# First loads, first weights, last stores: the two ends of a fused cross-covariance attention and MLP kernel rearranged

## The chip, the cores and the metric

The kernel runs on one core of a Trainium2 chip. A core has five engines that run their own instruction streams side by side and wait for each other through semaphores: TensorE (PE, matrix products), VectorE (DVE), ScalarE (ACT, pointwise functions), GpSimd (POOL) and SyncE (SP). Transfers are issued by SP, ACT or POOL and done by 16 DMA engines. The metric is the device time of a run in microseconds, and the number given is the median of the runs.

## The reference

Four batches of q, k and v, each 6080 tokens by 256 features, go through an attention over features, and its output through an MLP with 2048 hidden features:

```python
qn = q / (norm(q, axis=1) + 1e-6)          # over the 6080 tokens
kn = k / (norm(k, axis=1) + 1e-6)
s = kn.transpose(0, 2, 1) @ qn / tau       # 256 x 256 per batch
a = softmax(s, axis=-1)
x = (v @ a).reshape(24320, 256)
out = gelu_tanh(x @ w_in) @ w_out          # 256 -> 2048 -> 256
```

All inputs and the output are float32; `tau` is 1.

## The kernel before

**The algebra.** The norms are taken out of the product: G = q^T k is accumulated over the tokens ("gram"), the sums of squares of q's and k's columns are kept beside it, and the scores are G times a factor per row (from q) and per column (from k). Then v @ a @ w_in is computed as v @ (a @ w_in): A W_in is a 256 x 2048 matrix per batch (`AW`), so that the hidden layer is one product of v^T with it. v^T comes by DMA transposes of a bf16 copy of v (`cast_v`, L133, then `load_vt`, L143), apart from the first two blocks, whose v is turned on TensorE (`pe_vt`, L302).

**Blocks.** Each batch is cut into 12 blocks of 512 tokens (the last has 448), 48 in all (n = 0 to 47). A block computes eight pairs of hidden features: `g0` to `g7` are its products (`mm1`, L486), `G0` and so on their Gelu (`gelu`, L504); some pairs go through a scheme with fewer products (`small`, L544). The second product with w_out is also done with fewer products, on sums of w_out (`prep_wout`, `product`). The order of all this is written out by hand: `ORDER` holds lists of steps, one picked for each block by `WINDOW`, and each engine executes its own instructions in that order. A suffix such as `-1` or `+2` names another block than the current one.

**The start.** Only batch 0's attention can't hide behind other work. Its q and k are read in chunks of token rows: token row r of partition p is token p*47 + r, and a chunk of n rows has n x 128 tokens. Chunk 0 is loaded as float32 by SP and ACT and cast; the later ones are cast to bf16 by POOL's DMAs, one for q and one for k, each 512 KB of bf16 for 8 rows. The sizes are `[8, 7, 8, 8, 8, 6, 2]`, and the second chunk takes the 64 tokens that are left over. For each chunk ScalarE squares q, VectorE squares k, VectorE adds the halves of an 8-row chunk (`fold_rows`, L186), and TensorE sums the squares (`ss_rows`, L234): for q one narrow product per 128 columns and row, for k one 256-column product per row. Then come two 256-column gram products per row (`gram_row`, L219). Between these, `warm` (L341) issues products whose result nobody reads. `WARM` gives their number per chunk.

After the last chunk, `q_factor` (L269) has made q's factor, exp(-0.5 ln(sum of squares)), on ScalarE as soon as q's sums were there; `scores` (L278) makes k's factor in the same way (`lnk`, `rk`), multiplies G by it on VectorE (`S`), and takes the exponential on ScalarE with q's factor as scale (`eT`). `first_aw` (L315) makes the softmax sums and the first 512 features of `AW`; the remaining ones are `aw2` to `aw7`, with copies `ac2` to `ac7`, as steps of block 0. There `aw3` and `aw2` make features 512 to 1023, and need the second quarter of w_in. A load of ScalarE's table for Gelu (L856) follows `first_aw`.

**POOL's queue.** In order: the chunks of q and k, the first v, w_in in four loads of 512 features, the second v, both halves of w_out, then `vb2`, the bf16 copy of block 2's v. POOL's DMAs use eight completion semaphores in turn, so that each waits until the one eight before it has landed; each also waits for its buffer. q and k tiles have five buffers, the tiles of squares, which w_out's halves use too, have two.

**The end.** A block's output tile is stored by four DMAs of 32 partitions each, issued by SP (`store`, L784). The last block is stored in two halves (`store_half`, L773), each by two DMAs of SP and two of ACT. SP's and ACT's DMAs share eight completion semaphores in the same manner; the assignment is made when the program is built. SP's first DMA of block 46 waits for VectorE, its fourth for the semaphore that ACT's first DMA of block 47 uses.

## Time and profile before

| | |
|---|---|
| median of 3 runs | 701.26 us (700.62 to 702.35) |
| the profiled execution | 697.46 us, its span 695.7 us |
| TensorE's granted clock | 0.997 of full speed |
| batch 0's last q and k land | 32.8 and 33.4 us |
| first product of block 0 | 38.59 us |
| last product of block 47 | 688.8 us |
| HBM traffic over the span | 166 GB/s; the DMA engines are full until about 45 us |

Times in the profile are microseconds from the start of the span unless marked ns. In a row of a timeline stand the start, the duration, the engine, the line of the program, the operation, its output and inputs, how many instructions the row holds, and in brackets how long the engine sat idle before it and what released it. A merged row of several instructions overlaps the next where they are pipelined. `PEld` is TensorE's weight load, `SPq` and `ACTq` are DMAs issued by these engines, with the time of the issue only. A row of waits names who waited for whom, the time in all, how often and the longest. The first table of the page gives each engine's busy time; the chain of work that ended last follows the end of the program back from each step to what released it.

### The profile page before, as it was taken

How to read it: one execution, taken by the hardware profiler on the slowest of the kernel's cores; microseconds unless marked ns; L12 is line 12 of the kernel's file. 1: busy time of each engine (PE TensorE's matmuls, PEld its weight loads, DVE VectorE, ACT ScalarE, POOL GpSimd, SP SyncE). 2: the span in 40 equal slices, each digit the busy share in tenths (PEclk: the TensorE clock that was granted, in tenths of full speed). 3: DMA queues.
4: the chain of work that ended last, by engine and by line, in shares of the span. 5: the costliest groups of instructions: out<-in, count | busy, mean ns of one | idle time of the engine just before them, and what ended most of it. 6: DMA issues, size and time to landing. Idle time of an engine off the chain costs nothing.

```text
span 695.7 us, 14290 instructions
## 1 busy us (share of the span) xinstructions
PE 672.1 (97%) x5403; PEld 530.4 (76%) x5479; DVE 631.0 (91%) x1243; ACT 617.0 (89%) x894; POOL 70.2 (10%) x131
## 2 busy tenths in 40 slices
PE   3999999999999999999999999999999999999996
PEld 2756777777777777777777777777777888888885
DVE  4588899999998889999999889999999999999996
ACT  5379999998889999998888999999888999999993
POOL 4321100111001001101010010010000000000000
PEclk9999999999999999999999999999999999999998
DMA  9999996987777976657578787783553464453315
GB/s 243 208 260 130 149 153 120 122 113 95 119 132 120 122 129 113 111 81 128 87 135 121 120 133 119 95 135 58 77 107 62 77 103 73 76 96 59 60 32 88
DMA packets 162277, 79.32 MB, mean 114 GB/s; under 512 B 150464, under 2 KB 153280, under 8 KB 161216
## 3 DMA queue, kind: packets, MB, share of 16 engines
q0 software_dynamic: 13440, 39.46, 34.9%
q1 hardware_dynamic: 147664, 37.67, 33.9%
q10 hardware_dynamic: 1104, 1.28, 0.6%
q8 instruction: 43, 0.70, 0.4%
q14 instruction: 26, 0.21, 0.1%
HBM read 78.91 MB, written 36.83 MB: 166 GB/s over the span
## 4 chain that ended last, share of the span: by engine, by line
PE 89%; DMA 7%; DVE 1%; issue 1%; ACT 1%; POOL 0%; DVEq 0%; POOLq 0%; ACTq 0%
PE r L702 23%; PE h L496 19%; PE p L702 17%; PE rb L572 13%; PE qp L572 10%; PE G L227 5%; DMA t<-in_k_dram 2%; DMA vb<-in_v_dram 2%; DMA t<-in_q_dram 1%; PE awp L436 1%; DMA vT<-vb 1%; PE ss L259 0%; DVE qp L593 0%; PE rk L381 0%; DVE a L191 0%
## 5 line engine op out<-in xcount | busy, mean ns | idle before, releaser
L702 PEld LDWEIGHTS <-wcomb 128*128 128x128 bf16 x2688 | 262.4, 98 | 42.6 <-issue 0.2
L506 ACT ACTIVATE g<-h 128x1024 bf16<-128x1024 f32 (+1 forms) x178 | 179.5, 1013 | 16.1 <-PE h L496 14.2
L702 PE MATMUL r<-t,wcomb 128*128 128x256 bf16 (+1 forms) x1152 | 164.7, 271 | 0.1
L496 PE MATMUL h<-vT,aw 128*128 128x512 bf16 (+1 forms) x582 | 159.5, 376 | 3.5
L598 ACT ACTIVATE g<-qp 128x1024 bf16<-128x1024 f32 (+1 forms) x103 | 104.6, 1016 | 6.1 <-PE qp L572 3.7
L702 PE MATMUL p<-g,wcomb 128*128 128x256 bf16 (+1 forms) x760 | 106.7, 271 | 0.0
L496 PEld LDWEIGHTS <-aw 128*128 128x128 bf16 x712 | 69.4, 98 | 48.8 <-issue 0.7
L572 PEld LDWEIGHTS <-sw 128*128 128x128 bf16 x824 | 80.2, 98 | 27.5 <-issue 0.9
L178 ACT ACTIVATE sq<-t 128x1536 bf16<-128x1536 bf16 (+4 forms) x60 | 80.8, 1361 | 9.5 <-DMA t<-in_q_dram 9.5
L593 DVE TENSOR_TENSOR qp<-rb,yw 128x512 f32<-128x512 f32 (+1 forms) x103 | 71.0, 689 | 12.6 <-PE rb L572 8.6
L572 PE MATMUL rb<-tv,sw 128*128 128x256 bf16 (+1 forms) x412 | 78.0, 271 | 0.4 <-DVE qp L593 0.2
L596 DVE TENSOR_TENSOR xw<-rb,yw 128x512 f32<-128x512 f32 (+1 forms) x103 | 69.6, 676 | 4.6 <-PE rb L572 3.7
L572 PEld LDWEIGHTS <-aw 128*128 128x128 bf16 x618 | 60.4, 98 | 12.7 <-issue 1.2
L588 ACT ACTIVATE qp<-rb 128x512 f32<-128x512 f32 (+1 forms) x103 | 59.8, 580 | 10.4 <-PE rb L572 5.8
L591 ACT ACTIVATE yw<-qp 128x512 f32<-128x512 f32 (+1 forms) x103 | 61.2, 594 | 3.8 <-PE qp L572 2.1
L606 ACT ACTIVATE g<-xw 128x512 bf16<-128x512 f32 (+1 forms) x103 | 63.4, 626 | 1.3 <-DVE xw L596 1.2
L603 ACT ACTIVATE g<-rb 128x512 bf16<-128x512 f32 (+1 forms) x103 | 61.2, 596 | 3.7 <-PE rb L572 2.7
L675 DVE TENSOR_TENSOR t<-g,t 128x1024 bf16<-128x1024 bf16 (+1 forms) x96 | 63.7, 668 | 0.6
L677 DVE TENSOR_TENSOR t<-g 128x1024 bf16<-128x1024 bf16 (+1 forms) x96 | 64.0, 674 | 0.0
L679 DVE TENSOR_TENSOR t<-t,g 128x1024 bf16<-128x1024 bf16 (+1 forms) x96 | 63.6, 671 | 0.0
L227 PE MATMUL G<-t 128*128 128x256 bf16 x368 | 61.8, 279 | 0.1
L663 DVE TENSOR_TENSOR t<-g 128x2048 bf16<-128x2048 bf16 (+1 forms) x48 | 57.5, 1197 | 0.1
(124 smaller groups left out, 872.3 us busy)
## 6 DMA issues: line engine op xcount, KB each, us to landing
out_dram<-ot SPq DMA_DIRECT2D x176, 128.0 KB, 3.1
vb<-in_v_dram POOLq DMA_DIRECT2D x42, 256.0 KB, 4.5
t<-in_q_dram POOLq DMA_DIRECT2D x22, 384.0 KB, 4.9
t<-in_k_dram POOLq DMA_DIRECT2D x22, 384.0 KB, 6.3
wst<-in_moe_w_out_dram POOLq DMA_DIRECT2D x2, 1024.0 KB, 10.5
t<-in_q_dram POOLq DMA_DIRECT2D x3, 512.0 KB, 14.5
t<-in_k_dram POOLq DMA_DIRECT2D x3, 512.0 KB, 16.9
out_dram<-ot SPq DMA_DIRECT2D x12, 112.0 KB, 2.6
```

Source lines behind the costliest of these rows:

```text
L178: nc.scalar.activation(o, t[:np_, r, :], AF.Square)
L227: nc.tensor.matmul(G[b][:, jc, :], lhsT=qt[:np_, r, jc * 128 : jc * 128 + 128], rhs=kt[:np_, r, :], start=first and jc == 0, stop=jc == 1, ...
L496: mm = nc.tensor.matmul(hp[:, u, :cols], lhsT=AW[b][:, cc, fc * 128 : fc * 128 + 128], rhs=vt_tiles[n][:, cc, :cols], start=cc == 0, stop= ...
L506: nc.scalar.activation(gs(n)[:, 2 * p : 2 * p + 2, :cols], HP.pop((n, p))[:, :, :cols], AF.Gelu_apprx_tanh)
L572: GATE[0] = nc.tensor.matmul(acc[:, u * hc : u * hc + hc], lhsT=lhs[:, u * 128 : u * 128 + 128], rhs=rhs, start=m in (1, 5) and u == 0, st ...
L593: nc.vector.tensor_add(qp(n, i)[:, 1, :c], RB[n, i][:, :c], YW[n, i][:, :c])
L596: nc.vector.tensor_add(XW[n, i][:, :c], RB[n, i][:, :c], YW.pop((n, i))[:, :c])
L598: nc.scalar.activation(gs(n)[:, 2 * pa : 2 * pa + 2, :c].rearrange("p u (t x) -> p t u x", t=2), QP.pop((n, i))[:, :, :c].rearrange("p t ( ...
L675: nc.vector.tensor_sub(o, quarter(n, 1, 1, f0, f1), ts[1][:, f0:f1, :hc])
L677: nc.vector.tensor_sub(o, quarter(n, 1, 1, f0, f1), quarter(n, 0, 1, f0, f1))
L679: nc.vector.tensor_sub(o, ts[2][:, f0:f1, :hc], quarter(n, 1, 0, f0, f1))
L702: nc.tensor.matmul(ACCS[n, acc][:, :hc], lhsT=wcomb[:, w, fc, :], rhs=x, start=first and k == 0, stop=k == 3, skip_group_check=True)
```

## The change

In batch 0 the last two chunks, of 6 and 2 rows, become one of 8 rows, loaded in five pieces: q's rows 0 to 3, k's 0 to 4, k's 5 to 7, q's 4 and 5, q's 6 and 7. Squares and sums of that chunk follow the pieces; the chunk before it is not folded any more. q's factor is made inside `scores`, after k's. w_in arrives in two loads of 256 features and three of 512; `first_aw` computes its first 512 features as two parts of 256, the second in another PSUM tile. The first half of w_out is loaded ahead of the second v, the other half behind it. In block 0, `g0` stands before `aw3` and `aw2`. Of block 46's four stores POOL issues two. The other order lists and `WINDOW` change too (a list that was nearly the same as another is gone), but from block 1 on the instructions of TensorE, VectorE and ScalarE stand in the same order as before.

```diff
--- before.py
+++ after.py
@@ -73,7 +73,7 @@
 
 
     def chunks_of(b):
-        sizes = [8, 7, 8, 8, 8, 6, 2] if b == 0 else [6, 6, 6, 6, 6, 6, 6, 5]
+        sizes = [8, 7, 8, 8, 8, 8] if b == 0 else [6, 6, 6, 6, 6, 6, 6, 5]
         assert sum(sizes) == R
         res, r0 = [], 0
         for n in sizes:
@@ -127,6 +127,20 @@
     def load_qk(b, c):
         load_one(b, c, 0)
         load_one(b, c, 1)
+
+
+
+    PIECES = [(0, 0, 4), (1, 0, 5), (1, 5, 8), (0, 4, 6), (0, 6, 8)]
+
+    def load_last():
+        c = len(chunks_of(0)) - 1
+        r0, n = chunks_of(0)[c]
+        assert n == 8 and not with_rest(0, c)
+        qk_tiles[0, c] = [qkp.tile([128, 8, 256], BF16, tag="qk"[w], name=f"last{w}") for w in range(2)]
+        for w, a, e in PIECES:
+            nc.gpsimd.dma_start(
+                out=qk_tiles[0, c][w][:, a:e, :],
+                in_=(q, k)[w][0, 0 : R * 128, :].rearrange("(p r) c -> p r c", r=R)[:, r0 + a : r0 + e, :])
 
     v_bf = {}
 
@@ -179,9 +193,15 @@
             else:
                 nc.vector.tensor_mul(o, t[:np_, r, :], t[:np_, r, :])
 
-    def squares(b, c):
-        square(b, c, 0, "dve" if chunks_of(b)[c][1] <= 2 else "act")
-        square(b, c, 1, "dve")
+    def square_rows(c, which, a, e, eng):
+        if (0, c) not in SQ:
+            new_squares(0, c)
+        t = qk_tiles[0, c][which][:, a:e, :]
+        o = SQ[0, c][:, a:e, which * 256 : which * 256 + 256]
+        if eng == "act":
+            nc.scalar.activation(o, t, AF.Square)
+        else:
+            nc.vector.tensor_mul(o, t, t)
 
     def fold_rows(b, c):
 
@@ -231,26 +251,28 @@
                 start=first and jc == 0, stop=jc == 1,
                 skip_group_check=True)
 
-    def ss_rows(c, which):
+    def ss_rows(c, which, rows=None):
 
 
         last = c == len(chunks_of(0)) - 1
+        n = SQR.get((0, c), 8)
+        rows = range(n) if rows is None else rows
         if c == 0:
             SS[which] = pM.tile([128, 2] if which == 0 else [128, 256], FP32,
                                 tag="sp"[which], name=f"ss0{which}")
         sq = SQ[0, c]
-        n = SQR[0, c]
-        for r in range(n):
+        for r in rows:
+            end = last and r == n - 1
             if which == 0:
                 for jc in range(2):
                     nc.tensor.matmul(SS[0][:, jc : jc + 1],
                                      lhsT=sq[:, r, jc * 128 : jc * 128 + 128],
                                      rhs=ones_bf[:, 0:1],
                                      start=c == 0 and r == 0 and jc == 0,
-                                     stop=last and r == n - 1 and jc == 1)
+                                     stop=end and jc == 1)
             else:
                 nc.tensor.matmul(SS[1], lhsT=ones_bf, rhs=sq[:, r, 256:512],
-                                 start=c == 0 and r == 0, stop=last and r == n - 1)
+                                 start=c == 0 and r == 0, stop=end)
 
     def ss_cols(b):
 
@@ -266,27 +288,22 @@
 
     ET, RS = {}, {}
 
-    def q_factor():
+    def scores(b):
+
+        lnk = smx.tile([128, 256], FP32, tag="lnk")
+        nc.scalar.activation(lnk, SS[1], AF.Ln, bias=eps)
+        rk = smx.tile([128, 256], FP32, tag="rk")
+        nc.scalar.activation(rk, lnk, AF.Exp, scale=-0.5)
         lnq = smx.tile([128, 2], FP32, tag="lnq")
         nc.scalar.activation(lnq, SS[0], AF.Ln, bias=eps)
         rq = smx.tile([128, 2], FP32, tag="rq")
         nc.scalar.activation(rq, lnq, AF.Exp, scale=-0.5, bias=log_it)
-        RQ.append(rq)
-
-    RQ = []
-
-    def scores(b):
-
-        lnk = smx.tile([128, 256], FP32, tag="lnk")
-        nc.scalar.activation(lnk, SS[1], AF.Ln, bias=eps)
-        rk = smx.tile([128, 256], FP32, tag="rk")
-        nc.scalar.activation(rk, lnk, AF.Exp, scale=-0.5)
         S = smx.tile([128, 2, 256], FP32, tag="S")
         eT = smx.tile([128, 2, 256], BF16, tag="eT")
         for jc in range(2):
             nc.vector.tensor_mul(S[:, jc, :], G[b][:, jc, :], rk)
         for jc in range(2):
-            nc.scalar.activation(eT[:, jc, :], S[:, jc, :], AF.Exp, scale=RQ[0][:, jc : jc + 1])
+            nc.scalar.activation(eT[:, jc, :], S[:, jc, :], AF.Exp, scale=rq[:, jc : jc + 1])
         ET[b] = eT
 
     V0 = []
@@ -316,27 +333,34 @@
 
         b = 0
         AW[b] = awp.tile([128, 2, D], BF16, tag="aw", name=f"aw{b}")
-        ps = [pM.tile([128, 512], FP32, tag="sp"[ic], name=f"aw_ps{ic}") for ic in range(2)]
+        ps0 = [pM.tile([128, 256], FP32, tag="sp"[ic], name=f"aw_ps{ic}") for ic in range(2)]
+        ps1 = pH.tile([128, 2, 512], FP32, tag="b", name="aw_ps")
+        ps = [ps0, [ps1[:, ic, 0:256] for ic in range(2)]]
         sums = pM.tile([128, 2], FP32, tag="a", name="sums0")
         rs = smx.tile([128, 2], FP32, tag="rs")
         e = lambda jc, ic: ET[b][:, jc, ic * 128 : ic * 128 + 128]
+
+        def part(f, jc):
+            for ic in range(2):
+                nc.tensor.matmul(ps[f][ic], lhsT=e(jc, ic), rhs=win_bf[:, jc, f * 256 : f * 256 + 256],
+                                 start=jc == 0, stop=jc == 1)
+
         for jc in range(2):
             for ic in range(2):
                 nc.tensor.matmul(sums[:, ic : ic + 1], lhsT=e(jc, ic), rhs=ones_bf[:, 0:1],
                                  start=jc == 0 and ic == 0, stop=jc == 1 and ic == 1)
-            for ic in range(2):
-                nc.tensor.matmul(ps[ic], lhsT=e(jc, ic), rhs=win_bf[:, jc, 0:512],
-                                 start=jc == 0, stop=jc == 1)
+            part(0, jc)
         nc.vector.reciprocal(rs, sums)
         RS[b] = rs
+        part(1, 0)
+        part(1, 1)
         for f in range(2):
             for ic in range(2):
                 o = AW[b][:, ic, f * 256 : f * 256 + 256]
-                i = ps[ic][:, f * 256 : f * 256 + 256]
                 if (f, ic) == (0, 1):
-                    nc.scalar.activation(o, i, AF.Copy, scale=rs[:, ic : ic + 1])
+                    nc.scalar.activation(o, ps[f][ic], AF.Copy, scale=rs[:, ic : ic + 1])
                 else:
-                    nc.vector.tensor_scalar_mul(o, i, rs[:, ic : ic + 1])
+                    nc.vector.tensor_scalar_mul(o, ps[f][ic], rs[:, ic : ic + 1])
 
     def warm(n):
 
@@ -617,12 +641,11 @@
 
     WST = []
 
-    def load_wout():
-        for f in range(2):
-            w = sqp.tile([128, 8, 256], FP32, tag="sq", name=f"wst{f}")
-            WST.append(w)
-            nc.gpsimd.dma_start(out=w, in_=moe_w_out[f * 1024 : f * 1024 + 1024, :].rearrange(
-                "(t p) d -> p t d", p=128))
+    def load_wout(f):
+        w = sqp.tile([128, 8, 256], FP32, tag="sq", name=f"wst{f}")
+        WST.append(w)
+        nc.gpsimd.dma_start(out=w, in_=moe_w_out[f * 1024 : f * 1024 + 1024, :].rearrange(
+            "(t p) d -> p t d", p=128))
 
     def wc(i):
         return wcomb[:, i].rearrange("p f (b c) -> p (f b) c", c=32)
@@ -788,7 +811,8 @@
         ot = OT.pop(n)
         dst = out[r0 : r0 + cols, :].rearrange("(x t) (b c) -> b t x c", t=32, b=4)
         for bi in range(4):
-            nc.sync.dma_start(
+            eng = nc.gpsimd if n == NN - 2 and bi > 1 else nc.sync
+            eng.dma_start(
                 out=dst[bi],
                 in_=ot[bi * 32 : bi * 32 + 32, 0 : cols // 32].rearrange("p x h c -> p x (h c)"))
 
@@ -818,38 +842,55 @@
         win_bf = const.tile([128, 2, D], BF16)
         wcomb = const.tile([128, 7, 8, 128], BF16)
         nch = len(chunks_of(0))
-        WARM = [0, 4, 8, 8, 10, 2, 0]
-        for c in range(nch):
+        WARM = [0, 4, 8, 8, 10, 6]
+        for c in range(nch - 1):
             if c == 0:
                 cast_first(first)
             if c >= 3:
                 load_qk(0, c)
-            if 1 <= c < nch - 1:
+            if c == nch - 2:
+                load_last()
+            if c >= 1:
                 ss_rows(c - 1, 0)
                 ss_rows(c - 1, 1)
                 warm(WARM[c])
-            squares(0, c)
-            fold_rows(0, c)
-            if c == nch - 2:
-                ss_rows(c, 0)
-            if c == nch - 1:
-                ss_rows(c, 0)
-                q_factor()
-                ss_rows(c - 1, 1)
-                ss_rows(c, 1)
+            square(0, c, 0, "act")
+            square(0, c, 1, "dve")
+            if c < nch - 2:
+                fold_rows(0, c)
             for i in range(len(rows_of(0, c))):
                 gram_row(0, c, i)
+        c = nch - 1
+        ss_rows(c - 1, 1)
+        ss_rows(c - 1, 0)
+        warm(WARM[c])
+        square_rows(c, 0, 0, 4, "act")
+        ss_rows(c, 0, range(0, 4))
+        square_rows(c, 1, 0, 5, "dve")
+        for i in range(4):
+            gram_row(0, c, i)
+        ss_rows(c, 1, range(0, 5))
+        square_rows(c, 1, 5, 8, "dve")
+        square_rows(c, 0, 4, 6, "dve")
+        for i in (4, 5):
+            gram_row(0, c, i)
+        ss_rows(c, 1, range(5, 8))
+        ss_rows(c, 0, range(4, 6))
+        square_rows(c, 0, 6, 8, "dve")
+        for i in (6, 7):
+            gram_row(0, c, i)
+        ss_rows(c, 0, range(6, 8))
         wi = moe_w_in.rearrange("(c p) d -> p c d", p=128)
         load_v0(0)
-        for fs in range(4):
-            nc.gpsimd.dma_start(out=win_bf[:, :, fs * 512 : fs * 512 + 512],
-                                in_=wi[:, :, fs * 512 : fs * 512 + 512])
+        for f0, f1 in ((0, 256), (256, 512), (512, 1024), (1024, 1536), (1536, 2048)):
+            nc.gpsimd.dma_start(out=win_bf[:, :, f0:f1], in_=wi[:, :, f0:f1])
+        load_wout(0)
         load_v0(1)
-        load_wout()
+        load_wout(1)
         cast_v(2)
         warm(8)
+        pe_vt(0, "r")
         scores(0)
-        pe_vt(0, "r")
         pe_vt_copy(0, 0)
         pe_vt_copy(0, 1)
         first_aw()
@@ -929,21 +970,21 @@
 
 WINDOW = [
     0, 1, 2, 3, 4, 5, 6, 7, 8, 9, 10, 11, 12, 13, 14, 15, 16, 17, 18, 19, 20, 21, 22, 23,
-    24, 25, 26, 15, 16, 17, 27, 19, 20, 28, 29, 30, 31, 32, 33, 34, 35, 36, 37, 37, 38,
-    39, 40, 41,
+    24, 25, 26, 15, 16, 17, 18, 19, 20, 27, 28, 29, 30, 31, 32, 33, 34, 35, 36, 36, 37,
+    38, 39, 40,
 ]
 ORDER = [
-    """aw3 aw2 g0 ac3 lt+2 lv+3 g1 ac2 G0 aw5 G1 aw4 ac5 g2 lq+1 SW0 g3 G2 ac4 aw7 G3 aw6 ac7 g4
+    """g0 lt+2 lv+3 aw3 G0 aw2 ac3 g1 ac2 aw5 G1 aw4 lq+1 ac5 g2 SW0 g3 G2 ac4 aw7 G3 aw6 ac7 g4
     ac6 g5 T1a G4 lk+1 vtp G5 g6 vtc0 pA11 g7 G6 vtc1 T2a M1A G7""",
...
```

## The prediction

> **What bounds the kernel now.** I read the page's head and chain first, to see which engine sets the time, then the start and the end of the span, the only places where the change moves instructions.
>
> ```profile
> span 695.7 us, 14290 instructions
> PE 672.1 (97%) x5403; PEld 530.4 (76%) x5479; DVE 631.0 (91%) x1243; ACT 617.0 (89%) x894; POOL 70.2 (10%) x131
> PE 89%; DMA 7%; DVE 1%; issue 1%; ACT 1%; POOL 0%; DVEq 0%; POOLq 0%; ACTq 0%
> ```
>
> TensorE is busy 97% of the span and 89% of the chain that ended last. So a gain must either let TensorE reach the first block's stream earlier (and keep it earlier), or shorten what follows its last matmul. The start, from the timeline of TensorE and of ScalarE:
>
> ```profile
> 28.46 1.91 PE L227 MATMUL G<-t 128*128 128x256 bf16 x16
> 31.08 0.35 PE L246 MATMUL ss<-ones_bf,a 128*128 128x1 bf16 x8 [0.71 <-DVE a L191]
> 33.66 1.03 PE L252 MATMUL ss<-sq,ones_bf 128*128 128x256 bf16 x8
> 36.70 0.20 PE L325 MATMUL sums<-ones_bf,eT 128*128 128x1 bf16 x2 [0.26 <-ACT eT L289]
> 38.59 1.89 PE L496 MATMUL h<-vT_pe,aw 128*128 128x512 bf16 x8
> ```
>
> ```profile
> 34.13 0.29 ACT L273 ACTIVATE rq<-lnq,log_it 128x2 f32<-128x2 f32 x1
> 34.73 0.47 ACT L281 ACTIVATE lnk<-ss,eps 128x256 f32<-128x256 f32 x1 [0.30 <-PE ss L252]
> 36.14 0.91 ACT L289 ACTIVATE eT<-S,rq 128x256 bf16<-128x256 f32 x2 [0.49 <-DVE S L287]
> 38.37 1.28 ACT L856 ACT_TABLE_LOAD   x1
> ```
>
> The reader is to see that k's last factor starts when k's last sums end (34.69), that eT follows, and that from 31.08 on TensorE itself has next to no gap: it idles 0.26 us before 36.70. Then two rows that decide how much of a gain or loss at the start survives, and what the end waits for (timeline, then the waits of the DMA queues):
>
> ```profile
> 56.32 0.38 PE L572 MATMUL rb<-vT,aw 128*128 128x256 bf16 x2 [0.24 <-DMA vT<-vb]
> ```
>
> ```profile
> 688.92 1.92 ACTq L780 DMA_DIRECT2D out_dram<-ot  x4
> 690.66 0.32 SPq L791 DMA_DIRECT2D out_dram<-ot  x1
> 691.07 2.06 SPq L780 DMA_DIRECT2D out_dram<-ot  x4
> ```
>
> ```profile
> SPq L791 <- DMA out_dram<-ot: 5.4, 1, 5.4
> ```
>
> At 56.32 TensorE already waits 0.24 us for block 2's transposed v. At the end SP's fourth store of block 46 waits 5.4 us for a DMA, and block 47's four SP stores stand behind it.
>
> **The change, part by part.**
>
> *Loads.* Read issue by issue, before's chunk-4 k lands at 28.46 (issue plus time to landing), the next 384 KB of q at 30.24, of k at 32.07, then 128 KB of q at 32.82 and of k at 33.44. The new five pieces carry the same 1024 KB on the same queue, as 256 (q), 320 (k), 192 (k), 128 and 128 (q). Laid over the same curve they land at about 29.65, 31.15, 32.07, 32.82, 33.44. So k's last rows come 1.4 us earlier, and q's last come when k's last came. One more DMA costs POOL about 0.54 us of issue, long before it is due.
>
> *TensorE between 28.46 and k's last sum.* This is where I expect the gain to be lost. Chunk 4 is no longer folded: 8 sums of k instead of 4, 16 narrow ones of q instead of 8. It also takes warm 6 for 2. Its queue in program order is 16 gram, 8 k sums, 6 warm, 8 gram, 5 k sums, 4 gram, 3 k sums, that is 50 matmuls of 256 columns, and 16+8 narrow ones. Sixteen of the first kind take 1.91 us with the last one's tail, 0.1075 each start to start; eight narrow ones 0.21 (31.08 to the next group at 31.29), 0.027 each. 50 x 0.1075 + 24 x 0.027 = 6.02, so the last starts by 34.48 and ends near 34.68. Before, it ended at 34.69: the 0.71 us wait for the fold goes, and the added matmuls fill it. Each operand is there about a microsecond ahead of its turn (q's rows 4-6 land 32.82, used about 33.75), so earlier landings bring nothing. **Gain: 0.0.**
>
> *The q factor last.* ScalarE does lnk 34.72, rk (0.47 + 0.42 with gaps) to 35.64, then lnq and rq (0.26 and 0.29, 0.59 with gaps) to 36.28. Before, those two ran at 33.83 in ScalarE's idle time. VectorE's S takes 35.66 to 36.04, so rq ends last and eT starts at 36.28 for 36.14: **+0.15**. The gram of the last rows (done near 35.2) and v's transposes stay hidden.
>
> *A W_in in 256s, and the first block's order.* win's first 512 features land at 36.24 now; in halves, 35.5 and 36.24, both ahead of eT. The sums follow eT: rs at 37.77, the two 256-wide copies (0.42 on VectorE, 0.47 on ScalarE) end near 38.27, so block 0's g0 can start at 38.3, against 38.59. But now aw3 and aw2 (4 x 0.215 = 0.86) stand behind g0, where before they filled just this wait. g0, g1 and the two together are 1.72 + 0.86: TensorE reaches aw5 at 40.88, against 40.31: **+0.57**. Gelu gains nothing: ScalarE's copy ends near 38.3 as before, and the 1.28 us table load ends at 39.6 in both.
>
> *w_out around v.* The same bytes in another order: first w_out half at about 43.1 (3.0 us, by 41.45 to 44.43), second v at 44.45 for 41.45, second half at 47.4 as before. TensorE wants that v at 45.3, then 45.9: 1.4 us of cover. On POOL the first half waits for q's rows 4-6 to land and chunk 4's squares to be read (32.8), and holds the second v, the second half and vb2 behind it; vb2 then issues at 36.1 for 36.8, and lands at 48.5 as before, because the queue is full until then. **0**, and a microsecond per microsecond once v is later than 45.9.
>
> *What survives.* vT for block 2 comes from vb2 and is due at 56.27 in both. Before, TensorE waits 0.24 us there; coming 0.57 later, it does not. **Net at the start: +0.33.** An earlier TensorE could gain nothing past this point. From block 1 on, all engines keep the same order of work.
>
> *Stores over two queues.* SP and ACT take their eight completion semaphores in turn, and block 46's fourth store reuses that of ACT's first store of block 47 (688.92 plus 1.7 to landing: 690.62; the store goes at 690.66). With two stores on POOL this wait falls to block 47's second SP store: 690.66, the third 691.07, the fourth, waiting for ACT's second, about 691.5, against 692.67. That is -1.17; I take off 0.15 for SP and ACT now storing at the same time: **-1.0**. Between nothing (if the last to land were ACT's) and 1.2.
>
> Two rules of the Trainium skill bear on it. "SBUF — State Buffer", section "SBUF: two separate sides", warns that DMAs of the GpSimd queue starve while VectorE runs copies in its two-port mode, and in the section after it gives about 3.1 us for a DMA of 0.62. VectorE is busy 9.55 of the 10 us from 680 to 690. But its rows in the end are tensor_tensor and transposes, and POOL's vb issue at 49.44, across a 0.69 us VectorE cast, took 0.62 us against its usual 0.51 to 0.55. Even by the rule the two stores, ready at 683.8, would go by 690 and land, with 2.7 us, before the new end: 0 by both. "DMA: Bandwidth & Descriptors", "Issuing engines are not separate DMA queues", says a second issuing engine only saves the sequencer's issue time: two issues of 0.41 us, -0.8. The row says -1.0, because a wait moves too. I take the row.
>
> *Sum.* +0.33 - 1.0 = **-0.67**: span 695.7 to about 695.0. The profiled execution took 697.46 us, 3.8 under the median of the runs; nothing that the change touches is in that difference, so I set the same amount against the median: 701.26 - 0.67 = **700.6**.
>
> **The rivals.**
>
> *The start gains as the change reads.* If TensorE is not what paces 28.5 to 34.7 (for it: k's 1.4 us earlier; against it: the in-order sum above), eT comes up to 0.9 us earlier and aw5 0.2 to 0.4 earlier. Held by vT at 56.27, only 0.24 is kept: -1.25, 700.0. If vb2 and its transpose come earlier too, -1.4 to -2.3: 699 to 699.9.
>
> *The end gains nothing.* If the last store of ACT, or a POOL store that lands late, sets the end, only the start's loss is left: 701.6.
>
> *Slower: the second v behind w_out.* If the DMA engines let both halves of w_out pass, v lands with the second at 47.4, and TensorE stands 1.5 us at its transposes: 0.57 + 1.5 - 0.24 - 1.0 = +0.8, 702.1. It turns the sign once v lands after 46.6, and makes over 0.3% only after 47.9.
>
> **How the numbers follow.** 0.3% is 2.1 us, about what a measurement of this kernel can tell from no change. I give the forecast 0.45, the start's gain 0.27, no gain at the end 0.10, slower 0.18, in which I count losses at the start larger than my sum. Faster by over 0.3% needs nearly the full gain at both ends: 0.22, some of it from the forecast's own uncertainty. Slower by over 0.3% needs v or the first block over 3 us late: 0.18. That leaves 0.60. The range for 8 in 10 reaches both: 698.6 to 702.6.
>
> **What would show it.** Right: k's last sum ending near 34.7 with no wait ahead of it, rq ending after S, eT at 36.2 to 36.4, aw5 near 40.9, no wait for vT at 56, SP's last store near 691.5. Wrong: TensorE waiting for DMA before 34, eT before 35.8, a wait for v near 46, or SP's last store still near 692.7.

## The result and the profile after

The changed kernel takes 698.02 us (697.79 to 698.27, four runs), the kernel before on the same chip 701.81 (700.62 to 703.25): a ratio of 0.9945, 95% interval 0.9925 to 0.9966. It is 3.8 us faster, by more than the 0.3% that can be told apart. The forecast was 700.6 with a range of 698.6 to 702.6; the measured time lies below that range.

The two profiled executions say something else. The changed kernel's is an ordinary one of its runs, 698.27 us with a span of 696.4. That of before took 697.46 us with a span of 695.7, the best that this kernel was seen to do within 0.4 us. Compared by these two traces alone, the change loses 0.7 us. The page's head, engines and chain of the changed kernel:

```profile
span 696.4 us, 14330 instructions
PE 671.4 (96%) x5423; PEld 530.6 (76%) x5499; DVE 630.2 (90%) x1243; ACT 616.7 (89%) x894; POOL 73.1 (11%) x135
PE 92%; DMA 4%; DVE 1%; issue 1%; ACT 1%; POOL 0%; DVEq 0%; ACTq 0%; POOLq 0%
```

TensorE bounds it as before. The start, in the timelines of TensorE and of ScalarE:

```profile
28.66 1.91 PE L247 MATMUL G<-t 128*128 128x256 bf16 x16 [1.54 <-DMA t<-in_k_dram]
36.95 0.20 PE L350 MATMUL sums<-ones_bf,eT 128*128 128x1 bf16 x2
38.41 1.04 PE L520 MATMUL h<-vT_pe,aw 128*128 128x512 bf16 x3 [0.18 <-DVE aw L363]
56.62 0.38 PE L596 MATMUL rb<-vT,aw 128*128 128x256 bf16 x2
```

```profile
34.92 0.47 ACT L294 ACTIVATE lnk<-ss,eps 128x256 f32<-128x256 f32 x1 [3.95 <-PE ss L274]
36.02 0.29 ACT L300 ACTIVATE rq<-lnq,log_it 128x2 f32<-128x2 f32 x1
36.39 0.91 ACT L306 ACTIVATE eT<-S,rq 128x256 bf16<-128x256 f32 x2
38.35 1.28 ACT L897 ACT_TABLE_LOAD   x1
```

These rows are the forecast's: k's factor at 34.9 (34.7 forecast), q's factor last and eT behind it at 36.39 (36.28), g0 at 38.41 (38.3), the table load where it was, and no wait in brackets at 56.62. Most of it lies 0.1 to 0.2 later than forecast, because chunk 4's k came 0.2 later in this execution (28.66 for 28.46). One sign that the forecast had named as "wrong" is there, TensorE waiting 1.54 us for DMA at 28.66, but it costs nothing: in both kernels this product starts when chunk 4's k has landed, and only the products ahead of it ended earlier. The end: TensorE's last product of before and of the changed kernel, the changed kernel's stores, then SP's wait:

```profile
688.27 0.55 PE L702 MATMUL p<-g,wcomb 128*128 128x224 bf16 x4
```

```profile
689.22 0.55 PE L725 MATMUL p<-g,wcomb 128*128 128x224 bf16 x4
688.38 0.68 POOL L815 DMA_DIRECT2D out_dram<-ot  x1 [2.66 <-issue]
689.87 3.46 SPq L803 DMA_DIRECT2D out_dram<-ot  x4
689.87 1.93 ACTq L803 DMA_DIRECT2D out_dram<-ot  x4
```

```profile
SPq L803 <- DMA out_dram<-ot: 1.8, 1, 1.8
```

SP's wait of 5.4 us has become one of 1.8, as was meant. But TensorE's last product ends at 689.77 for 688.82, and from there to the end of the span it takes 6.64 us for 6.87. So a quarter of a microsecond came from the stores, where 1.0 was forecast. SP's last store goes at 692.9, the other sign of "wrong" ("still near 692.7"): it is 0.74 earlier counted from the last product, which is 0.95 later.

Nothing in these rows makes 3.8 us. What does is not in the profiled execution of before. In five further comparisons before ran 136 times (and once more, at 2531 us, which is left out): between 697.1 and 703.4 us, with 43 of the runs above 700. The changed kernel's four times lie within 0.5 us. That before's four runs here were all above 700.6, as one in four of the 136 was, makes the 3.8 us larger than usual: the 136 have a median of 698.9, only 0.9 above the changed kernel. Whether that is chance or the chip is not shown. The question is what makes before so uneven, and which part of the change takes that away.

### The profile page after: what moved, and what is told of

It reads as the page before. It is cut to its first block, busy times and chain, and to the rows that moved or that the text cites. A ratio compares the mean times of both kernels' runs of the same rounds, so it can differ in the third digit from the quotient of the medians.

```text
span 696.4 us, 14330 instructions
## 1 busy us (share of the span) xinstructions
PE 671.4 (96%) x5423; PEld 530.6 (76%) x5499; DVE 630.2 (90%) x1243; ACT 616.7 (89%) x894; POOL 73.1 (11%) x135
## 4 chain that ended last, share of the span: by engine, by line
PE 92%; DMA 4%; DVE 1%; issue 1%; ACT 1%; POOL 0%; DVEq 0%; ACTq 0%; POOLq 0%
PE r L725 23%; PE h L520 21%; PE p L725 17%; PE rb L596 13%; PE qp L596 10%; PE G L247 5%; DMA t<-in_k_dram 3%; PE awp L460 2%; DMA t<-in_q_dram 1%; PE ss L281 0%; DVE xw L620 0%; PE ss L274 0%; PE warm L369 0%; PE rk L405 0%; DVE t L686 0%
## 5 line engine op out<-in xcount | busy, mean ns | idle before, releaser
L192 ACT ACTIVATE sq<-t 128x1536 bf16<-128x1536 bf16 (+4 forms) x59 | 79.3, 1359 | 7.3 <-DMA t<-in_q_dram 7.3
L612 ACT ACTIVATE qp<-rb 128x512 f32<-128x512 f32 (+1 forms) x103 | 59.7, 580 | 10.4 <-PE rb L596 5.8
L247 PE MATMUL G<-t 128*128 128x256 bf16 (+1 forms) x352 | 58.1, 273 | 1.5 <-DMA t<-in_k_dram 1.5
## 6 DMA issues: line engine op xcount, KB each, us to landing
wst<-in_moe_w_out_dram POOLq DMA_DIRECT2D x2, 1024.0 KB, 10.5
```

The source lines that it names most:

```text
L192: nc.scalar.activation(o, t[:np_, r, :], AF.Square)
L247: nc.tensor.matmul(G[b][:, jc, :], lhsT=qt[:np_, r, jc * 128 : jc * 128 + 128], rhs=kt[:np_, r, :], start=first and jc == 0, stop=jc == 1, ...
```

## The experiments

Of each kernel ten runs were timed. Ratios are to before on the same chip, in the same rounds; since before is uneven, a median of the kernel itself often tells more than its ratio. "vT2" is block 2's transposed v, for which TensorE waits at 56 us, and `rb` its first product there; "vb2" the bf16 copy that it is made from; "vb4" the copy of block 4's v, the DMA that POOL issues next to it.

| | edit | median (range) | ratio, 95% |
|---|---|---|---|
| a | before again | 699.75 (697.92 to 704.23) | 1.001 (0.999 to 1.004) |
| b | stores only | 701.86 (699.69 to 704.45) | 1.003 (1.001 to 1.006) |
| c | all but the stores | 698.18 (697.84 to 699.57) | 0.998 (0.997 to 1.000) |
| d | first batch only | 702.01 (699.24 to 703.75) | 1.004 (1.002 to 1.006) |
| e | all but the order lists | 697.59 (697.24 to 699.21) | 0.998 (0.996 to 1.000) |
| f | all but w_out around v | 697.99 (697.78 to 699.04) | 0.998 (0.996 to 1.000) |
| g | before, vb4 6 us later | 697.22 (696.76 to 697.61) | 0.998 (0.996 to 0.999) |
| h | before, vT2 used 7 us later | 698.08 (697.53 to 699.33) | 0.998 (0.996 to 0.999) |
| i | w_in only | 697.52 (697.06 to 703.63) | 0.999 (0.997 to 1.001) |
| j | all but w_in | 699.24 (698.99 to 699.61) | 1.000 (0.998 to 1.002) |
| k | e, vb4 6 us later | 697.71 (697.46 to 697.86) | 0.998 (0.996 to 0.999) |
| l | g, and the stores | 697.82 (697.51 to 698.31) | 0.998 (0.997 to 0.999) |
| m | changed kernel, vb4 earlier | 699.00 (697.85 to 702.04) | 0.999 (0.997 to 1.002) |
| n | before, vb4 1.3 us later | 696.95 (696.75 to 697.20) | 0.997 (0.995 to 0.999) |
| o | g, and w_in | 697.11 (696.82 to 697.59) | 0.997 (0.995 to 0.999) |
| p | g, and the first batch | 697.85 (697.54 to 698.02) | 0.996 (0.994 to 0.998) |
| q | g, and the order lists | 697.52 (697.38 to 697.84) | 0.996 (0.994 to 0.998) |

**The parts one by one (a to d).** a is before, unedited. b has only the stores' edit, c everything else, d only the new first batch (cut to its core):

```diff
-            nc.sync.dma_start(
+            eng = nc.gpsimd if n == NN - 2 and bi > 1 else nc.sync
+            eng.dma_start(
```

```diff
-        sizes = [8, 7, 8, 8, 8, 6, 2] if b == 0 else [6, 6, 6, 6, 6, 6, 6, 5]
+        sizes = [8, 7, 8, 8, 8, 8] if b == 0 else [6, 6, 6, 6, 6, 6, 6, 5]
...
+    PIECES = [(0, 0, 4), (1, 0, 5), (1, 5, 8), (0, 4, 6), (0, 6, 8)]
```

> The kernel before, unchanged, to see its usual execution in a trace: the one profiled took 697.5 us, the median of its runs is 701.8. Whatever costs the other 4 us should show as a stretch that is longer than in the first trace. Start theory (a transfer of the first 60 us is late in most executions and TensorE waits for it): a new TensorE wait of 3 to 4 us before 60 us, last matmul at 692 to 693 us. End theory (the chain of stores after the last matmul is longer in most executions): last matmul at 689 as before, 3 to 4 us more behind it. Ratio to before 1.000 by both.

> The kernel before with only block 46's last two stores moved to POOL. End theory: nearly all of the change's 3.8 us, 698.0 to 698.6. Start theory: only the 1.0 us of the forecast, 700.8 (between 700.4 and 701.2). SP's last store in both by 691.5 to 692, counted from a last matmul at 688.8.

> The changed kernel with all of block 46's stores back on SP. End theory: little or nothing left of the gain, 701.5 to 702.2 (the start alone loses 0.3 to 0.9). Start theory: most of it, 698.8 to 699.5, that is 1.0 us over the changed kernel.

> The kernel before with only the last chunk of the first batch changed (five pieces, k ahead of q's last rows, q's factor at the last, v's transposes ahead of the scores); w_in in four loads, w_out behind v, the first block's order and the stores as before. By the forecast's sum it loses 0.15 us at eT and gains nothing: 701.6 to 702.3. Start theory: if the last chunk's loads are what is late in most executions, 698.5 to 699.5 (a gain of 2.5 us or more); if it is w_in, w_out or the order of the first block, 701 to 702 as in the forecast.

The stores alone gain nothing, b is even 0.3% slower, and without them the gain is all there (c: 698.18, with one run of 699.6). The first batch alone is as uneven as before, and slower. The trace of a caught a short run (697.94), with a wait of 0.81 us for vT2. But the trace of b, one of its long executions (703.16), shows the place. In the timeline of TensorE:

```profile
38.31 1.02 PE L436 MATMUL awp<-win_bf,eT 128*128 128x512 bf16 x4 [0.31 <-DMA win_bf<-in_moe_w_in_dram]
59.61 0.49 PE L572 MATMUL rb<-vT,aw 128*128 128x256 bf16 x2 [2.95 <-DMA vT<-vb]
59.90 1.06 PE L702 MATMUL p<-g,wcomb 128*128 128x256 bf16 x4
60.76 3.08 PE L496 MATMUL h<-vT_pe,aw 128*128 128x512 bf16 x8
63.67 0.60 PE L702 MATMUL r<-t,wcomb 128*128 128x256 bf16 x4
```

and TensorE in stretches (the length, TensorE's busy time and instructions, its granted clock, the DMA share, GB/s):

```profile
50.00:56.00 6.00, 5.95 (x37) 1.00 1.25 122
60.00:62.00 2.00, 2.00 (x8) 0.50 1.13 225
62.00:64.00 2.00, 2.00 (x10) 0.71 1.38 66
64.00:66.00 2.00, 2.00 (x19) 1.00 1.21 92
```

TensorE waits 2.95 us for vT2, and then works at half its clock until about 63.2: four products of 256 columns take 1.06 us for 0.60. From `rb` to its last product b takes 634.18 us, where undisturbed kernels take 632.5: 1.7 more. Ahead of `rb`, from chunk 4's gram on, it takes 31.00 us where g (below, without the wait) takes 27.42. Of these 3.58 us, 0.43 come from w_in's second quarter, which is late at 38.31, and the other 3.15 are the wait: it costs about 0.2 more than its bracket says, since rows of TensorE overlap where nothing waits (at 63.67 a row of 0.60 us, and the next starts 0.44 later). By the same count the first profile's wait of 0.24 us costs 0.44 (27.86 us for 27.42), and b's costs 3.15 and 1.7, together 4.8.

The Trainium skill has the rule for the clock ("TensorE: Matmul & The Clock Gate", "What's actually happening": it falls to half after an idle window of about 3.4 us and needs as long a busy one to come back). The half clock lasts as long here, from 59.7 to 63.2. But the idle time before the product was 2.95, so by measurement less is enough; a's wait of 0.81 us left the clock at 1.00.

**Is it that wait? (e to h).** e and f each take one part out of the changed kernel. e has the order lists of before (of which the first lines are shown), f w_out's old place:

```diff
-    """g0 lt+2 lv+3 aw3 G0 aw2 ac3 g1 ac2 aw5 G1 aw4 lq+1 ac5 g2 SW0 g3 G2 ac4 aw7 G3 aw6 ac7 g4
+    """aw3 aw2 g0 ac3 lt+2 lv+3 g1 ac2 G0 aw5 G1 aw4 ac5 g2 lq+1 SW0 g3 G2 ac4 aw7 G3 aw6 ac7 g4
```

```diff
-        load_wout(0)
         load_v0(1)
+        load_wout(0)
         load_wout(1)
```

g and h leave before as it is and take only the wait away, in two ways. g issues vb4 (`lv+3`) later; h uses vT2 (`vs+1`, `w0m1+1`) some 7 us later. Both in block 1's list:

```diff
-    """g0 pF0-1 lt+2 lv+3 M1B-1 G0 pS1-1 g1 pF1-1 M5A-1 G1 M5B-1 g2 pS2-1 cq-1 lq+1 T2b-1 g3 G2
+    """g0 pF0-1 lt+2 M1B-1 G0 pS1-1 g1 pF1-1 M5A-1 G1 M5B-1 g2 pS2-1 cq-1 lq+1 T2b-1 g3 G2
-    pS4-1 M6A-1 G3 M6B-1 pS3-1 g4 y5-1 g5 ap-1 G4 T1a M3A-1 G5 w0m1+1 M3B-1 T3b-1 lk+1 g6
+    pS4-1 M6A-1 G3 M6B-1 pS3-1 g4 y5-1 g5 lv+3 ap-1 G4 T1a M3A-1 G5 w0m1+1 M3B-1 T3b-1 lk+1 g6
```

```diff
-    pS4-1 M6A-1 G3 M6B-1 pS3-1 g4 y5-1 g5 ap-1 G4 T1a M3A-1 G5 w0m1+1 M3B-1 T3b-1 lk+1 g6
-    pA12-1 vs+1 g7 G6 c12-1 T3a-1 M7B-1 G7 T4a-1 M2B-1 M2A-1 T4b-1 pNA-1 M7A-1 w0m5+1 ax-1""",
+    pS4-1 M6A-1 G3 M6B-1 pS3-1 g4 y5-1 g5 ap-1 G4 T1a M3A-1 G5 M3B-1 T3b-1 lk+1 g6
+    pA12-1 g7 G6 c12-1 T3a-1 M7B-1 G7 T4a-1 vs+1 M2B-1 M2A-1 T4b-1 pNA-1 M7A-1 w0m1+1 w0m5+1 ax-1""",
```

> The changed kernel with the order lists of before: aw3 and aw2 ahead of g0, and block 0's later loads paced by later matmuls. Theory now: TensorE's wait for block 2's transposed v, which before can land 3 us late, is what the change removes. If the order of block 0 does it, the spread returns: median 1 to 3 us over the changed kernel, single runs up to 702 to 703. If w_out or w_in does it, the runs stay within 1 us of each other, at or up to 0.5 us under the changed kernel (TensorE comes 0.57 us earlier).

> The changed kernel with the second v ahead of both halves of w_out, as before. If the order of w_out and v is what keeps block 2's transposed v in time: spread and median as the kernel before. If not: as the changed kernel, within 0.3 us, since the same bytes stand ahead of block 2's v.

> The kernel before with one step moved: the load of block 4's v (bf16 copy, DRAM to DRAM) issues after g5 of block 1 and not after g0, about 6 us later. If block 2's transposed v is late because it stands behind that load's large packets on the DMA engines: no wait at 56, it lands by 54 to 55.5, runs within 1 us of each other and about 697.3, that is 1.5 us or more under the kernel before. If the cause is another: spread and median as before.

> The kernel before with block 2's first products (and its sums of v on VectorE) moved some 7 us later in block 1's list, nothing else. If the time that differs between runs is TensorE's wait for block 2's transposed v: spread gone, median 697 to 697.7, better than both kernels. If it lies elsewhere: spread and median as before.

g and h both end the runs of 700 and more. g's ten runs lie within 0.9 us, at 697.22, which beats the changed kernel too. h has two runs of 699.3, and the trace is of one of them: vT2 lands 10.5 us after its issue, late enough that VectorE still waits 1.3 us for it. e and f stay steady, but for one run each of 699.2 and 699.0: neither the order nor w_out's place is what does it.

**Which part (i, j).** i has w_in's edit alone, with `first_aw` in two parts, j everything but it:

```diff
-        for fs in range(4):
-            nc.gpsimd.dma_start(out=win_bf[:, :, fs * 512 : fs * 512 + 512],
-                                in_=wi[:, :, fs * 512 : fs * 512 + 512])
+        for f0, f1 in ((0, 256), (256, 512), (512, 1024), (1024, 1536), (1536, 2048)):
+            nc.gpsimd.dma_start(out=win_bf[:, :, f0:f1], in_=wi[:, :, f0:f1])
```

> The kernel before with only w_in's first quarter in two loads of 256 features and A W_in computed in two parts. So far every kernel with these five loads is steady, and block 2's bf16 v lands at 48.1 to 48.7; of those with four loads three of six traces have it at 49.7 to 50.0. If the loads of w_in decide that: steady runs (within 1.5 us of each other), median 697.3 to 698.2. If they do not: spread and median of the kernel before.

> The changed kernel with w_in in four loads again and A W_in's first 512 features in one part. If w_in's loads decide: the spread is back, single runs over 701, median 1 us or more over the changed kernel's 698.1. If block 0's order and w_out's place are enough without it: within 0.3 us of the changed kernel.

i is still uneven (three runs of ten at 698.9, 700.8 and 703.6), j is steady (its 699.24 has another cause, at the end of the program: below). So none of the three parts tried alone (stores, first batch, w_in) ends the wait, and the changed kernel less one part does, whichever is left out (c, e, f and j; the first batch was never the one). That suggests a common quantity behind them. In the traces it is the distance between two issues: SP issues vT2's transpose as soon as vb2 has landed, POOL issues vb4 when TensorE has done block 1's g0. Where vb4 follows closely, vT2 lands late (one execution of each kernel):

| | a | before | i | d | b | h | e | f | c | after | j | g |
|---|---|---|---|---|---|---|---|---|---|---|---|---|
| vb4's issue after vT2's, us | 0.96 | 0.92 | 1.04 | -0.07 | 0.33 | 0.09 | 1.40 | 1.44 | 1.46 | 1.66 | 1.82 | 7.3 |
| vT2 lands after, us | 8.4 | 7.8 | 8.0 | 7.3 | 9.9 | 10.5 | 6.0 | 6.0 | 6.0 | 6.9 | 6.1 | 6.1 |

**Cause or companion? (m, n).** m takes the distance from the changed kernel and leaves all its parts; n gives before the smallest step of distance and none of the parts. The edit of m stands first, to the changed kernel's list, then that of n, to the list of before:

```diff
-    """g0 pF0-1 lt+2 lv+3 M1B-1 G0 g1 pS1-1 pF1-1 G1 M5A-1 M5B-1 cq-1 g2 pS2-1 lq+1 T2b-1 g3 G2
+    """lv+3 g0 pF0-1 lt+2 M1B-1 G0 g1 pS1-1 pF1-1 G1 M5A-1 M5B-1 cq-1 g2 pS2-1 lq+1 T2b-1 g3 G2
```

```diff
-    """g0 pF0-1 lt+2 lv+3 M1B-1 G0 pS1-1 g1 pF1-1 M5A-1 G1 M5B-1 g2 pS2-1 cq-1 lq+1 T2b-1 g3 G2
+    """g0 pF0-1 lt+2 M1B-1 G0 pS1-1 g1 lv+3 pF1-1 M5A-1 G1 M5B-1 g2 pS2-1 cq-1 lq+1 T2b-1 g3 G2
```

> The changed kernel, with block 4's copy of v issued one step earlier in block 1's list, ahead of the block's first products: about 0.9 us earlier, so that it follows the transpose of block 2's v by some 0.8 us where it now follows by 1.66. Theory (the distance between the two issues decides whether the transpose lands in 6 us or in 7 to 10): the transpose lands 7 us or more after its issue, TensorE waits for it at 56 us in some executions, and the median is 698.5 to 700.5 with single runs over 700. Rival (it is the first batch or w_in, by what they move in the DMA queues): 698.0 with all ten runs within 1.5 us, as the changed kernel was, the transpose landing in 6 to 7 us.

> The kernel before, with block 4's copy of v one pair of products later (behind g1 instead of g0 in block 1): about 0.9 to 1.3 us later, so 1.9 to 2.2 us behind the transpose of block 2's v instead of 0.9. Theory: the smallest dose is enough, the transpose lands within 6.5 us, no wait at 56 us, all runs between 696.7 and 698, median 697.2 to 697.7, like the run with 6 us. Rival (a full 5 us is needed for other reasons than the two DMAs meeting): as before, 698.5 with single runs of 700 and more.

Both came out as the distance theory says. With all parts of the change but vb4 early, the long runs are back (700.3, 701.7 and 702.0 among the ten; the trace is of a shorter one, in which vT2 lands at 56.1, in time); with none of them and vb4 1.3 us later, the ten runs lie within 0.45 us, at 696.95, the best of all. The timeline of m, with the two issues at the same time:

```profile
48.81 6.11 SPq L162 DMA_TRANSPOSE vT<-vb  x2
48.82 0.50 POOL L152 DMA_DIRECT2D vb<-in_v_dram  x1 [1.65 <-PE h L520]
```

The timeline of n, with 1.45 us between them and no wait at `rb`:

```profile
49.47 4.89 SPq L148 DMA_TRANSPOSE vT<-vb  x2
50.92 0.50 POOL L138 DMA_DIRECT2D vb<-in_v_dram  x1 [4.24 <-PE h L496]
56.10 0.38 PE L572 MATMUL rb<-vT,aw 128*128 128x256 bf16 x2
```

The issues of DMAs, with the time from issue to landing last, of before at 48.5:

```profile
vT<-vb SPq DMA_TRANSPOSE x1, 7.8
```

of m at 48.8:

```profile
vb<-in_v_dram POOLq DMA_DIRECT2D x1, 256.0 KB, 6.2
vT<-vb SPq DMA_TRANSPOSE x1, 7.3
```

and of n at 49.5:

```profile
vT<-vb SPq DMA_TRANSPOSE x1, 6.0
```

In n vT2 is issued a microsecond later than in before, lands at 55.5, and TensorE finds it there at 56.10; in before it landed at 56.3. Between a distance of 1.04 and 1.40 us lies the point where it turns in these traces; the changed kernel's own 6.9 us, at 1.66, lies between the two groups. In the changed kernel vb4 comes at 50.14 for 49.44, while vT2 is issued at the same time as before (48.48 for 48.52). Counted from chunk 4's k, which is 0.2 later there, TensorE reaches vb4 0.5 later, the very loss that the forecast had found at the start, and vb2 lands 0.24 sooner.

**What the parts cost without the wait (k, l, o, p, q).** l, o, p and q each add one part to g, by the edits shown above (the stores, w_in, the first batch, the changed kernel's order lists); k is e with g's edit of block 1's list.

> The changed kernel with the order lists of before and with block 4's v loaded after g5 of block 1. If the two gains add (0.5 us from TensorE coming earlier to block 0's stream, steadiness from the late load): 696.6 to 697.2, all runs within 1 us, better than the kernel before and than the changed one. If the late load is worth nothing once w_in is in halves: 697.4 to 697.7.

> The kernel before with block 4's v loaded late (steady, 697.2) and two of block 46's stores on POOL. The forecast's step for the stores: -1.0, 696.2. From the trace of the changed kernel, where ACT's first store of block 47 takes 2.1 us to land and not 1.7: -0.3, 696.9. No gain: 697.2.

> The kernel before, with block 4's copy of v 6 us later and w_in beginning with two loads of 256 features (the first A W_in in two parts). With the wait for block 2's v away, what the first part alone is worth shows: by the profile g0 can begin 0.2 to 0.3 us earlier, so 696.8 to 697.1 against 697.2 with the later copy alone. Rival (w_in's first features land ahead of the softmax in any case, or a DMA more costs as much): 697.2 to 697.6.

> The kernel before with the new first batch (last 8 rows in five pieces, no fold of the chunk before, q's factor at the last) and block 4's copy of v 6 us later. With the wait at 56 us away the start shows alone. By the prediction's sum: the earlier k is worth 0.0 and q's factor costs 0.15, so 0.1 to 0.2 over the later copy alone, 697.2 to 697.5. Rival (the five pieces delay what follows on the DMA queue, as the 1.5 us later copy of block 2's v in the run with the first batch alone suggests, and TensorE loses it somewhere): 697.7 or more, with single runs over 698.

> The kernel before with the changed kernel's order lists (block 0's first products ahead of A W_in's aw3 and aw2) and block 4's copy of v 6 us later. By the prediction's sum TensorE loses 0.57 at the start and, with no wait to take it up, keeps it to the end: 697.5 to 697.8. Rival (some later wait takes it up): 697.2, as with the later copy alone.

No part gains when it is added to g alone: against g's 697.22, w_in stands at -0.1, the order at +0.3, the first batch at +0.6, the stores at +0.6; g, l, o and the last two come from four comparisons, so a tenth or two between them means nothing. l and p missed their forecasts (696.2 to 697.2 and 697.2 to 697.5), and so did k: 697.71 where 696.6 to 697.2 was hoped for, so the late copy brings e, which is steady already, nothing. The traces tell where. Since chunk 4's k lands within 28.2 to 28.9 from one execution to the next, the stages are counted from the product that waits for it:

| us | before | g | n | q: order | p: first batch | o: w_in | l: stores | after |
|---|---|---|---|---|---|---|---|---|
| chunk 4's gram to block 2's `rb` | 27.86 | 27.42 | 27.43 | 28.01 | 27.57 | 27.57 | 27.42 | 27.96 |
| `rb` to the end of the last product | 632.50 | 632.49 | 632.51 | 632.49 | 633.15 | 632.50 | 632.51 | 633.15 |
| from there to the end of the span | 6.87 | 6.88 | 6.80 | 6.84 | 6.93 | 6.83 | 7.61 | 6.64 |

The first row has the forecast's start: +0.59 for the order (forecast 0.57), +0.15 for the first batch (0.15). Together the parts make +0.54, and +0.62 without the halves of w_in (j: 28.04), so the two losses do not add up in full. The second row has a loss that nobody counted: 0.66 us in every traced kernel with the first batch, at places that are the same in p and in the changed kernel: 0.36 at 331 us, 0.24 at 593, 0.06 before. The waits of TensorE's weight loads in g:

```profile
PEld L572 <- issue: 1.7, 7, 0.4
```

and in p:

```profile
PEld L589 <- issue: 2.2, 9, 0.4
```

These are pauses in which the engine waited for nothing that the profile shows: seven of 0.24 us on average at this line in g, nine in p. Why it makes two more is open.

The third row has the stores. SP's last wait of the program, in before:

```profile
SPq L1181 <- PEq L1181: 0.7, 2, 0.5
```

and in l:

```profile
SPq L1182 <- PEq L1182: 1.8, 2, 1.3
```

In l, as in b and j, this wait is 1.0 to 1.2 us longer (j: 7.80 us from the last product to the end), and takes more than the stores win; in the changed kernel it is 0.8, but there POOL's second store sat 2.66 us with no cause shown. In l POOL's two stores go one right behind the other, with VectorE doing the same work, so VectorE's work alone is not what holds the second:

```profile
683.70 1.36 POOL L792 DMA_DIRECT2D out_dram<-ot  x2 [56.69 <-DVE ot L727]
```

The traces sort by w_in: with the stores on POOL and w_in in five loads (the changed kernel, e, f, k, m) the end takes 6.6 to 6.7 us, with the stores and four loads (b, j, l) 7.6 to 7.8, without the stores 6.8 to 7.0 either way. So the stores lose 0.7 by themselves and win 0.2 beside the five loads. How one acts on the other was not found.

## Why the prediction was wrong

*The sum's transfer to the runs* is the step that failed. "The profiled execution took 697.46 us, 3.8 under the median of the runs; nothing that the change touches is in that difference". What is in it is vT2's wait in the other executions, and the change removes that wait. The wait stood in the forecast, as 0.24 us at 56.32, and it was even found that TensorE's delay takes it up. What was not asked is how large this wait is in the executions whose time was to be forecast. In b's long execution it is 2.95 us, and 4.8 with the half clock behind it; before's median of 701.8 lies 4.6 above the 697.2 that before takes without it (g). No long execution of before itself was traced: that its long runs are this wait rests on g, h and n, which end them, and on m, which brings them back.

*Loads, TensorE between 28.46 and k's last sum, the q factor last:* right. The earlier k brought nothing, q's factor cost 0.15 (p: 27.57 for 27.42).

*A W_in and the first block's order:* right, 0.54 measured for the whole start, 0.57 forecast.

*w_out around v:* right, without effect (f: 697.99 for 698.02). One figure of the rival on it does not follow from its own terms: over 0.3%, 2.1 us, needs v at 48.7, since 0.57 + 2.8 - 0.24 - 1.0 makes 2.1, and not at 47.9. Nothing hangs on it.

*What survives:* the net +0.33 took off 0.24 for the wait, as its bracket has it, but the wait cost 0.44. So between the two profiled executions the start loses only 0.10 (27.96 for 27.86). Against a before without the wait it costs its full 0.54.

*From block 1 on, the same order:* the instructions keep their order, but 0.66 us of pauses came with the first batch. That cost was not in the sum.

*Stores over two queues:* a size was off. From the last product to SP's last store it takes 3.12 us for 3.86, a gain of 0.74 for the 1.17 forecast: ACT's first store of block 47, with SP storing beside it, lands in 2.1 us where 1.7 was taken, and SP's second waits for it. From that store to the end of the span it then takes 3.5 us for 3.0, where the sum took off 0.15, so that 0.24 of the forecast 1.0 is left.

*The sum:* in this measure 0.54 + 0.66 - 0.24 = +0.96 against g's trace, and the medians say 698.0 for 697.2, +0.8. So by its own parts the change is a loss, and its gain is a side effect: it happens to keep vb4 away from vT2. The forecast had the sign right by luck, from a gain at the end that was mostly not there.

*The rivals:* the first came nearest in the time, 699 to 699.9 if vb2 and its transpose come earlier, but for a reason that did not occur: k's early rows gained nothing, and vb2 landed as before. Only its transpose came earlier, 55.4 for 56.3. The second's end ("only the start's loss is left") is half of what happened. The third's v was not late.

That c, e and f, the change less one part each, gain only 0.2% beside the 0.55% of its own comparison has the same cause: they gain what before loses by the wait, and before's median was 701.8 in that comparison, 698.5 to 700.5 in the others.

## What to carry to other kernels

When the profiled execution is far from the median of the runs, the difference is work that the kernel does in the other executions: look first at the waits that are barely there, since one of 0.24 us in a good execution may be one of 3 us in a bad one. Before a transfer that TensorE waits for, keep the next large copy a good microsecond away: here one step moved in a list (n) brought 696.95 us for the change's 698.02, and held all runs within 0.45 us. Cost each part against a version from which that wait is taken away; otherwise its noise hides parts that lose 0.3 to 0.6 us each.

## What was not expected of the hardware

A transpose of 512 tokens (as many as the 256 KB copy beside it) issued 1.4 us or more ahead of that copy from DRAM to DRAM landed in 6.0 to 6.9 us, issued less than 1.1 us ahead of it or after it in 7.3 to 10.5. The table of before has the DMA engines full until about 45 us; they are so here too, with a share of 1.11 from 45 to 60 us for 1.20 from 30 to 45. The DMA packets in the traces show how the two transfers meet. The copy is 16 packets of 16 KB, the transpose 1024 of 256 bytes. In before the copy's packets start between 53.5 and 54.0 us and take 1.9 us each on average; from 54 to 55 us only 16 packets of transposes start, where it was 538 in the microsecond before, and in g, whose copy comes later, 599 in the same one. In b single packets of the copy take up to 5.4 us, and from 53 to 59 us no more than 250 packets of transposes start in any microsecond. In the stretches (packets count where they start, with their whole time), before, then g:

```profile
53.00:54.00 1.00, 1.00 (x11) 1.00 2.62 400
54.00:55.00 1.00, 0.95 (x5) 1.00 0.02 4
```

```profile
53.00:54.00 1.00, 1.00 (x9) 1.00 1.11 241
54.00:55.00 1.00, 1.00 (x7) 1.00 1.31 252
```

The Trainium skill ("DMA: Bandwidth & Descriptors", "Queues, rings and completion order") says that each DMA engine takes turns between its queues by whole packets, and a transpose held behind the copy's large packets fits that. The traces do not say which engine a packet ran on, so the turns themselves are not shown.

Why POOL's loads run a microsecond or more behind in some executions (vb2 lands at 49.5 to 50.0 in b, d, h and n, at 48.2 to 49.0 in the others) is open. The delay is there once w_in has landed, at 41.1 to 41.6 us for 39.7 to 40.7. It brings vT2's issue nearer to vb4's, and only n, which keeps 1.45 us between them, does not pay for it.
